# Strided attention with an expert layer on one core: the first sixteen weight loads issued as four loads of 32 partitions each

## The chip, the cores and the metric

The kernel runs on one core of one Trainium2 chip. The metric is the device time of one execution in microseconds (us). Before the change three runs took 869.03, 870.39 and 871.68 us; their median, 870.39 us, is the time that the change is held against.

## What is computed

```python
# q, k, v: (8, 8, 576, 64) float32;  w_in: (512, 2048), w_out: (2048, 512), both float64
scores = (1/8) * q @ k.T                      # per batch and head
mask   = local band of 32      for heads 0..3
         same position mod 32  for heads 4..7    # both causal
attn   = softmax(where(mask, scores, -1e9));  x = (attn @ v) -> (4608 tokens, 512)
h = x @ w_in;  g = h * clip(h + 3, 0, 6) / 6;  out = g @ w_out
```

The weights arrive as 8-byte numbers, so a block of 128 rows by 512 columns is 512 KB in memory.

## The kernel before

All work is written as operations of a planner (class `Plan`): each has an engine, an estimated cost, a due time and the tiles that it reads and writes. `emit` simulates the engines with these numbers and fixes the order in which each engine issues its operations; on the chip every engine then runs its list strictly in that order, waiting on semaphores where an input is not there yet.

A batch is worked on as four pairs of heads (`pair`). Batch 0 goes first: q and k are loaded (L491), turned upright by TensorE (L371), scores (L600, L608), softmax on DVE, POOL and ACT, and the product with v (L388, L735) gives x. The v loads of batch 0 are made of small pieces (L377, L380, L566). From batch 1 on q and k are loaded in 32-row strips (L357) and transposed by DVE (L533). The expert layer of batch 0 (`ffn(0)`) starts as soon as x and the first weights are there: `first_product` (L856 to L858) makes `ph`, ACT and DVE apply the gate (L776, L779), ACT and POOL split the result in a high and a low part (L790, L794), and `mm2` (L833 to L835) adds into `acc`. Later batches use a scheme with fewer products, on the same weights.

The weights come in 32 blocks (`weight_part`, k = 0 to 31): four of w_in (`rawi`), four of w_out (`rawo`), four of w_in and so on. Each is loaded by one DMA on SP's queue (`load`, L273) into a tile of 128 partitions by 1024 32-bit words. ACT then reads it twice (`high` L281, `low` L285), DVE joins the parts (`join` L289), and ACT or POOL write the high part (L303, L305) and POOL the low part (L308). The same place is reused for the result. The first sixteen blocks (k < 16) are loaded early: four before the v loads of the second and fourth pair, the other twelve right behind these; behind the twelve, SP issues the q and k strips of batch 1.

Each DMA of SP tells its landing on one of eight semaphores, taken in turn (DMAHW0 to DMAHW7 in the orders below). SP issues a DMA only when the one that used this semaphore before, eight DMAs earlier, has landed. The DMAs of SP that are issued stand in line for the core's 16 DMA engines.

The lines that fix a weight load:

```python
raw = new(wp, key, [P, TOK, 2], I32, f"raw{name}")
nc.sync.dma_start(raw, src.bitcast(I32).rearrange("p (n t) -> p n t", t=2))
...
op("SP", 0.53, load, writes=[key], due=..., early=7.0 if k < 16 else due - 30.0, ...)
```

Of the kernel before, what the change touches and what calls it, by code (L numbers as in the profile page):

```python
# [12 lines left out]
I32 = mybir.dt.int32  # L13
# [6 lines left out]
P = 128  # L20
# [9 lines left out]
TOK = 512  # L30
TURNS = ((0, 2, 1, 3), (2, 0, 3, 1)) + ((0, 2, 1, 3),) * 6
AHEAD = 27.0
OPEN = 6.0
HIENG = {"ACT": 0.63, "POOL": 0.7}

# [24 lines left out]
class Plan:  # L60
# [12 lines left out]
    def op(self, engine, us, fn, reads=(), writes=(), due=0.0, room=0.0, mode="", after=0.0, take=None, give=None, early=0.0):  # L73
        n = len(self.ops)
        before = set()
        for k in reads:
            if k in self.wrote:
                before.add(self.wrote[k])
            self.used.setdefault(k, []).append(n)
        for k in writes:  # L80
            if k in self.wrote:
                before.add(self.wrote[k])
            before.update(self.used.pop(k, ()))
            self.wrote[k] = n
        before.discard(n)
        how = engine if isinstance(engine, dict) else {engine: us}
        self.ops.append((how, fn, before, due, room, mode, after, take, give, early))
        return n
# [85 lines left out]
def attention_ffn(ctx: ExitStack, tc, q, k, v, w_in, w_out, out):  # L174
    nc = tc.nc
# [21 lines left out]
    op = plan.op  # L197
    tiles = {}

    def new(pool, key, shape, dtype, name):  # L200

        tag = "_".join(str(x) for x in key)
        t = tiles[key] = pool.tile(shape, dtype, tag=tag, name=name)
        return t
# [52 lines left out]
    def wkey(w, g, i):  # L257
        return ("w", w, g, i)

    def weight_part(k, w, g, i):  # L260
        key = wkey(w, g, i)
        fc = FQ * g if w == "i" else FQ * g + i + 1
        due = T0 + fc * TILE / NFC - 5.0 + 0.01 * k
        fkey = ("x", 1, 1 - (k // 2 % 2 if k < 20 else 0), k % 2)
        name = f"{w}{g}{i}"

        def load():
            if w == "i":
                src = w_in[i * P:(i + 1) * P, g * TOK:(g + 1) * TOK]
            else:  # L270
                src = w_out[(g * FQ + i) * P:(g * FQ + i + 1) * P, :]
            raw = new(wp, key, [P, TOK, 2], I32, f"raw{name}")
            nc.sync.dma_start(raw, src.bitcast(I32).rearrange("p (n t) -> p n t", t=2))  # L273

        def bits():
            raw = tiles[key]
            return raw.rearrange("p n t -> p (n t)")[:, :TOK]

        def high():
            f = new(xp, fkey, [P, TOK], I32, f"f{name}")  # L280
            nc.scalar.activation(f.bitcast(F32), tiles[key][:, :, 1].bitcast(F32), AF.Prelu, scale=2.0 ** -112, alpha=2.0 ** 32)  # L281

        def low():
            raw = tiles[key].bitcast(U16).rearrange("p n (t u) -> p n t u", u=2)[:, :, 0, 1]
            nc.scalar.activation(bits(), raw, AF.Copy, scale=2.0 ** -13, bias=2.0 ** -14 - 0.5)  # L285

        def join():
            f = tiles[fkey]
            nc.vector.scalar_tensor_tensor(out=f, in0=f, scalar=3, in1=bits(),  # L289
                                           op0=ALU.logical_shift_left, op1=ALU.bitwise_or)  # L290

        def whole():
            f = tiles[fkey].bitcast(F32)
            return f if w == "i" else f.rearrange("p (h e d) -> p h d e", h=2, d=2)

        def part(x):
            t = tiles[key][:, x]
            return t if w == "i" else t.rearrange("p (h d e) -> p h d e", h=2, d=2)

        def hi(e):  # L300
            new(wp, key, [P, 2, TOK], F32R, f"w{name}")
            if e == "ACT":
                nc.scalar.copy(part(0), whole())  # L303
            else:
                nc.gpsimd.tensor_copy(part(0), whole())  # L305

        def lo():
            nc.gpsimd.tensor_tensor(out=part(1), in0=whole(), in1=part(0).bitcast(F32), op=ALU.subtract)  # L308

        op("SP", 0.53, load, writes=[key], due=-49 + 0.01 * k if k < 4 else -48.4 + 0.01 * k if k < 6 else -2 + 0.1 * k if k < 16 else due - 20.0, early=7.0 if k < 16 else due - 30.0, after=1.6 if k < 16 else 1.25)  # L310
        op("ACT", 0.68, high, reads=[key], writes=[fkey], due=due - 5, room=LATE + 1.0)
        op("ACT", 0.68, low, writes=[key], due=due - 5)
        op("DVE", 1.05, join, reads=[key], writes=[fkey], due=due - 3)
        op(HIENG, 0, hi, reads=[fkey], writes=[key], due=due - 2)
        op("POOL", 1.3, lo, reads=[fkey, key], writes=[key + ("lo",), key], due=due - 1)
# [124 lines left out]
    def pair(g):  # L440
# [37 lines left out]
        for x in "qk":  # L478
# [55 lines left out]
            op("SP", 3.4 if b > 4 else 2.8, load, writes=[nkey], due=due - 35, early=due - 45, after=2.0)  # L534
            op("DVE", 0.8 if loc else 1.25, tr, reads=[nkey, "plain"], writes=[tkey[x]], due=due - 18, early=max(due - AHEAD, T0 + OPEN), room=LATE)

# [1002 lines left out]
    for n, part in enumerate(parts):  # L1539
        weight_part(n, *part)  # L1540
# [63 lines left out]
```

## Time and profile before

| | |
|---|---|
| median of three runs | 870.39 us (869.03 to 871.68) |
| the profiled execution, its own time | 871.98 us |
| its span, first to last instruction | 870.2 us |
| TensorE (PE) busy | 847.4 us, 97% of the span |
| DVE, ACT, POOL busy | 539.0, 558.9, 616.6 us |
| moved by DMA | 179.12 MB, mean 206 GB/s |

The rows of the profile are from the profiled execution, and its 871.98 us is 1.59 us above the median. PE is matrix multiplication, PEld its weight load, SPq the queue of DMA issues on SyncE. A row of the timeline is a run of like instructions on an engine: start, length, engine, line, operation, output and input, count, and in brackets the idle time before it with what ended that. The length of an SPq row is the time that issuing took, not the transfer.

### The profile page before, as it was taken

The page shows a single profiled execution, that of the slowest core. Times are in us where ns is not written, and L with a number is a line of the kernel's source. Part 1 is how long each engine was busy: PE and PEld are TensorE (multiplying, and loading weights), DVE is VectorE, ACT ScalarE, POOL GpSimd, SP SyncE. Part 2 cuts the span into 40 slices and gives each one's busy share as a digit, 9 for nine tenths or more (in the row PEclk, how much of TensorE's full clock was granted, in tenths as well). Part 3 has the DMA queues.
Part 4 walks back from the last instruction along what each step waited for, and adds up shares of the span by engine and source line. Part 5 has one row for each costly group of instructions (what it writes and reads, how often), then busy time and mean ns, then how long its engine had stood idle before and what let it go on. Part 6 is the DMA issues. An engine that isn't in the chain of part 4 may idle for free.

```text
span 870.2 us, 18946 instructions
## 1 busy us (share of the span) xinstructions
PE 847.4 (97%) x6962; PEld 683.8 (79%) x6962; DVE 539.0 (62%) x898; ACT 558.9 (64%) x1246; POOL 616.6 (71%) x606
## 2 busy tenths in 40 slices
PE   8889999999999999999999999999999999999996
PEld 6667777887888788888888878788888778888884
DVE  5688878344454538454546664466767888555586
ACT  3687657678778865877677965776744645454441
POOL 4688877587547799766676994465975987767673
PEclk9999999999999999999999999999999999999998
DMA  8968723898984455898999897877666667866636
GB/s 194 330 138 233 234 41 73 210 281 245 279 234 108 128 129 141 233 266 233 269 277 289 274 301 214 237 204 189 183 202 193 185 180 222 240 202 192 183 122 145
DMA packets 323308, 179.12 MB, mean 206 GB/s; under 512 B 182864, under 2 KB 300368, under 8 KB 323216
## 3 DMA queue, kind: packets, MB, share of 16 engines
q1 hardware_dynamic: 318564, 176.27, 71.5%
q10 hardware_dynamic: 4652, 1.64, 0.9%
q8 instruction: 55, 0.90, 0.4%
q14 instruction: 37, 0.30, 0.1%
HBM read 136.97 MB, written 40.89 MB: 204 GB/s over the span
## 4 chain that ended last, share of the span: by engine, by line
PE 82%; DMA 5%; POOL 5%; DVE 4%; ACT 2%; issue 1%; SPq 0%; POOLq 0%; DVEq 0%; ACTq 0%
PE P L1129 8%; PE P L1130 8%; PE P L1131 8%; PE cP L1452 5%; PE cP L1453 5%; PE cP L1454 5%; PE acc L833 5%; PE ph L856 5%; PE ph L857 4%; PE ph L858 4%; PE acc L835 4%; PE acc L834 4%; PE acc L1214 3%; PE acc L1215 3%; PE acc L1216 3%; PE pv L399 2%
## 5 line engine op out<-in xcount | busy, mean ns | idle before, releaser
L1470 DVE SCALAR_TENSOR_TENSOR C<-cP,C 128x512 f32<-128x512 f32 x96 | 65.7, 687 | 40.4 <-PE cP L1454 39.5
L794 POOL TENSOR_TENSOR gl<-u,gh 128x512 fp32r<-128x512 f32 x48 | 65.2, 1361 | 33.3 <-ACT gh L790 17.1
L1141 DVE TENSOR_TENSOR G<-P,G 128x512 f32<-128x512 f32 x64 | 44.0, 689 | 65.6 <-PE P L1131 53.2
L1129 PE MATMUL P<-B_T,wr 128*128 128x512 f32 x192 | 76.1, 396 | 3.9 <-ACT G L1136 2.3
L833 PE MATMUL acc<-wo,gh 128*128 128x512 f32 x192 | 77.2, 402 | 0.0
L835 PE MATMUL acc<-wo,gl 128*128 128x512 f32 x192 | 75.2, 392 | 0.3 <-POOL gl L794 0.2
L834 PE MATMUL acc<-wo,gh 128*128 128x512 f32 x192 | 74.9, 390 | 0.0
L1130 PE MATMUL P<-B_T,wr 128*128 128x512 f32 x192 | 74.8, 390 | 0.0
L1131 PE MATMUL P<-B_T,wr 128*128 128x512 f32 x192 | 74.8, 390 | 0.0
L1136 ACT COPY G<-P 128x512 f32<-128x512 f32 x64 | 37.6, 587 | 52.2 <-PE P L1131 51.7
L1367 POOL TENSOR_TENSOR sp<-G,sp 128x512 fp32r<-128x512 f32 x34 | 47.6, 1411 | 24.6 <-ACT sp L1363 22.5
L665 POOL TENSOR_TENSOR e<-e,st 128x144 f32<-128x144 f32 (+1 forms) x64 | 44.9, 704 | 20.7 <-DVE st L661 15.2
L779 DVE SCALAR_TENSOR_TENSOR u<-u,ph 128x512 f32<-128x512 f32 x48 | 32.8, 684 | 38.0 <-ACT u L776 37.8
L856 PE MATMUL ph<-x,wi 128*128 128x512 f32 x128 | 52.5, 410 | 2.3 <-ACT x L426 1.2
L857 PE MATMUL ph<-x,wi 128*128 128x512 f32 x128 | 50.8, 397 | 1.4 <-DVE x L429 0.8
L700 ACT COPY atloc<-e 32x192 f32<-32x192 f32 x144 | 50.8, 353 | 1.9 <-DVE e L690 0.3
L776 ACT ACTIVATE u<-ph,three 128x512 f32<-128x512 f32 x48 | 33.0, 687 | 28.1 <-PE ph L858 27.8
L858 PE MATMUL ph<-x,wi 128*128 128x512 f32 x128 | 50.8, 397 | 0.0
L644 DVE TENSOR_REDUCE st<-e 128x8 f32<-128x144 f32 (+1 forms) x64 | 25.6, 412 | 35.8 <-POOL e L640 35.6
L1129 PE MATMUL P<-B_B,wr 128*128 128x512 f32 x120 | 47.1, 392 | 0.0
L1130 PE MATMUL P<-B_B,wr 128*128 128x512 f32 x120 | 46.8, 390 | 0.0
L1129 PEld LDWEIGHTS P<-B_T,wr 128*128 128x128 f32 x192 | 36.0, 188 | 13.7 <-ACT G L1136 3.6
(604 smaller groups left out, 2672.6 us busy)
## 6 DMA issues: line engine op xcount, KB each, us to landing
wr<-dA SPq DMA_DIRECT2D x72, 256.0 KB
or<-do SPq DMA_DIRECT2D x32, 512.0 KB
wr<-dSu SPq DMA_DIRECT2D x48, 256.0 KB
wr<-dSv SPq DMA_DIRECT2D x48, 256.0 KB
or<-do SPq DMA_DIRECT2D x48, 256.0 KB
rawi<-in_moe_w_in_dram SPq DMA_DIRECT2D x16, 512.0 KB
rawo<-in_moe_w_out_dram SPq DMA_DIRECT2D x16, 512.0 KB
do<-wo SPq DMA_DIRECT2D x16, 512.0 KB
```

The lines of the kernel that those rows point to most:

```text
L700: nc.scalar.copy(at[PAD * (a + h):PAD * (a + h) + PAD, :, rows], e[rows, :, PAD * h:PAD * h + PAD])
L794: (nc.vector if tail else nc.gpsimd).tensor_tensor(out=to, in0=src(), in1=tiles[gk[0]].bitcast(F32), op=ALU.subtract)
L833: nc.tensor.matmul(acc, gh, woh, start=fc == 0, stop=False)
L834: nc.tensor.matmul(acc, gh, wol, start=False, stop=False)
L835: nc.tensor.matmul(acc, gl, woh, start=False, stop=end)
L856: nc.tensor.matmul(ph, wih, xh, start=n_ == 0, stop=False)
L857: nc.tensor.matmul(ph, wih, xl, start=False, stop=False)
L858: nc.tensor.matmul(ph, wil, xh, start=False, stop=n_ == NCC - 1)
L1129: nc.tensor.matmul(ph, wh, xh, start=fresh and k == 0, stop=False, skip_group_check=not fresh)
L1130: nc.tensor.matmul(ph, wh, xl, start=False, stop=False, skip_group_check=not fresh)
L1131: nc.tensor.matmul(ph, wl, xh, start=False, stop=k == 1, skip_group_check=not fresh)
L1470: nc.vector.scalar_tensor_tensor(out=tiles[ck], in0=tiles[bank], scalar=1.0 / 6.0, in1=tiles[ck], op0=ALU.mult, op1=ALU.add)
```

## The change

`CHOP = 4` is new. For the first sixteen weight blocks the load is a loop over four quarters of 32 partitions, each a DMA of its own (128 KB instead of 512 KB). For the other sixteen blocks `step` is 128 and one DMA is issued as before. The planner's cost of a load on SP goes from 0.53 to 1.6 us for these sixteen.

```diff
+CHOP = 4
...
             raw = new(wp, key, [P, TOK, 2], I32, f"raw{name}")
-            nc.sync.dma_start(raw, src.bitcast(I32).rearrange("p (n t) -> p n t", t=2))
+            step = P // CHOP if k < 16 else P
+            for p0 in range(0, P, step):
+                nc.sync.dma_start(raw[p0:p0 + step], src[p0:p0 + step].bitcast(I32).rearrange("p (n t) -> p n t", t=2))
...
-        op("SP", 0.53, load, writes=[key], due=..., early=7.0 if k < 16 else due - 30.0, after=1.6 if k < 16 else 1.25)
+        op("SP", 0.4 * CHOP if k < 16 else 0.53, load, writes=[key], due=..., early=7.0 if k < 16 else due - 30.0, after=1.6 if k < 16 else 1.25)
```

Lines below the loop move down by three (L273 is L276 after, L357 is L360). Line and buffer numbers aside, the lists of PE, DVE, ACT and POOL are the same, row for row, before and after; on SP the only rows that differ are the sixteen loads.

On SP, the first four weight loads and what stands behind them; `rawi00` is the block of w_in with group 0 and row block 0, `v0_10` and `v0_3` are v tiles of batch 0. Before:

```order
L566 DMA v0_2_242<-in_v_dram 18x2x512 x4
L273 DMA rawi00_333<-in_moe_w_in_dram 128x1024
L273 DMA rawi01_335<-in_moe_w_in_dram 128x1024
L273 DMA rawi02_357<-in_moe_w_in_dram 128x1024
L273 DMA rawi03_359<-in_moe_w_in_dram 128x1024
L377 DMA v0_10_260<-in_v_dram 32x64
```

and after:

```order
L569 DMA v0_2_242<-in_v_dram 18x2x512 x4
L276 DMA rawi00_333<-in_moe_w_in_dram 32x1024 x4
L276 DMA rawi01_358<-in_moe_w_in_dram 32x1024 x4
L276 DMA rawi02_403<-in_moe_w_in_dram 32x1024 x4
L276 DMA rawi03_429<-in_moe_w_in_dram 32x1024 x4
L380 DMA v0_10_260<-in_v_dram 32x64
```

Four issues have become sixteen, in the same place.

On SP, the end of the twelve later loads and the strips of batch 1 (`qn1_2`, `kn1_2`: third pair), with the semaphores that each issue waits for. Before:

```order
L273 DMA rawo12_591<-in_moe_w_out_dram 128x1024 [waits DMAHW2_49]
L273 DMA rawo13_597<-in_moe_w_out_dram 128x1024 [waits DMAHW3_49]
L357 DMA qn1_2_692<-in_q_dram 32x18x32 [waits DMAHW4_49,PE_49]
L357 DMA qn1_2_692<-in_q_dram 32x18x32 [waits DMAHW5_49]
L357 DMA qn1_2_692<-in_q_dram 32x18x32 [waits DMAHW6_49]
L357 DMA qn1_2_692<-in_q_dram 32x18x32 [waits DMAHW7_49]
L357 DMA kn1_2_730<-in_k_dram 32x18x32 [waits DMAHW0_49,PE_49]
```

and after:

```order
L276 DMA rawo13_934<-in_moe_w_out_dram 32x1024 [waits DMAHW2_49]
L276 DMA rawo13_934<-in_moe_w_out_dram 32x1024 [waits DMAHW3_49]
L360 DMA qn1_2_953<-in_q_dram 32x18x32 [waits DMAHW4_49,PE_49]
L360 DMA qn1_2_953<-in_q_dram 32x18x32 [waits DMAHW5_49]
L360 DMA qn1_2_953<-in_q_dram 32x18x32 [waits DMAHW6_49]
L360 DMA qn1_2_953<-in_q_dram 32x18x32 [waits DMAHW7_49]
L360 DMA kn1_2_982<-in_k_dram 32x18x32 [waits DMAHW0_49,PE_49]
```

The strips keep their semaphores (48 more DMAs are six full turns of the eight), but the eight DMAs ahead of them are now two blocks, where they were eight.

On ACT, the first readers of a weight block. Before:

```order
L720 COPY at64_195<-pe0_01_582 128x288 [waits PE_49]
L281 ACTIVATE fi00_680<-rawi00_333 128x512 [waits DMAHW2_49]
L285 ACTIVATE rawi00_333<-rawi00_333 128x512 [waits Activation_49]
L281 ACTIVATE fi01_689<-rawi01_335 128x512 [waits DMAHW3_49]
L426 CAST x0_00_702<-pv0_00_638 128x288 [waits PE_49]
```

and after:

```order
L723 COPY at64_195<-pe0_01_579 128x288 [waits PE_49]
L284 ACTIVATE fi00_683<-rawi00_333 128x512 [waits DMAHW4_49,DMAHW5_49,DMAHW3_49,DMAHW2_49]
L288 ACTIVATE rawi00_333<-rawi00_333 128x512 [waits Activation_49]
L284 ACTIVATE fi01_697<-rawi01_358 128x512 [waits DMAHW6_49,DMAHW7_49,DMAHW1_49,DMAHW0_49]
L429 CAST x0_00_705<-pv0_00_636 128x288 [waits PE_49]
```

A reader waits for four landings where it waited for one; the same holds for DVE's `join` and POOL's first writer.

## Rows read from the trace of the kernel before

**Rows 1.** The windows view: three stretches of the span. Columns: stretch, its length, busy us of PE, PEld, DVE, ACT, POOL (instructions), granted TensorE clock as a share of full speed, mean busy share of the 16 DMA engines, GB/s that they moved.
```profile
0.00:60.00 60.00, 51.18 (x927) 38.93 (x928) 41.03 (x92) 36.44 (x81) 36.02 (x60) 0.94 0.84 231
60.00:860.00 800.00, 794.25 (x6030) 643.57 (x6029) 494.62 (x803) 522.48 (x1166) 580.57 (x547) 1.00 0.72 205
```
**Rows 2.** The waits view for PE in the first 60 us: instruction that waited, what it waited for, us in total, times, longest.
```profile
PE ps L600 <- issue: 2.5, 2, 1.3
PE pe L371 <- issue: 2.1, 1, 2.1
PE ph L856 <- ACT x L426: 1.2, 1, 1.2
PE ph L857 <- DVE x L429: 0.8, 2, 0.5
```
**Rows 3.** The timeline of SP's queue, merged and in narrow windows: weight loads, v loads and strips. Columns: start us, us that issuing took, then the DMA and its count.
```profile
16.95 2.10 SPq L273 DMA_DIRECT2D rawi<-in_moe_w_in_dram  x4
19.09 0.68 SPq L377 DMA_DIRECT2D v<-in_v_dram  x1
28.02 0.32 SPq L566 DMA_DIRECT2D v<-in_v_dram  x1
28.38 1.77 SPq L273 DMA_DIRECT2D rawo<-in_moe_w_out_dram  x4
34.70 0.33 SPq L273 DMA_DIRECT2D rawo<-in_moe_w_out_dram  x1
35.92 0.33 SPq L273 DMA_DIRECT2D rawo<-in_moe_w_out_dram  x1
38.77 9.25 SPq L357 DMA_DIRECT2D qn<-in_q_dram  x4
50.81 0.50 SPq L357 DMA_DIRECT2D kn<-in_k_dram  x1
53.83 0.52 SPq L366 DMA_DIRECT2D vloc<-in_v_dram  x1
60.56 1.95 SPq L357 DMA_DIRECT2D qn<-in_q_dram  x4
```
**Rows 4.** The waits view for SP's queue from 16 to 48 us (columns as in group 2).
```profile
SPq L273 <- DMA rawo<-in_moe_w_out_dram: 3.6, 4, 1.5
SPq L357 <- DMA rawi<-in_moe_w_in_dram: 3.0, 3, 1.2
```
**Rows 5.** The windows view again (columns as in group 1).
```profile
10.00:12.00 2.00, 2.00 (x67) 2.00 (x64) 1.13 (x2) 1.31 (x3) 0.00 (x0) 1.00 0.87 214
24.00:28.00 4.00, 3.17 (x85) 2.95 (x89) 2.06 (x5) 1.59 (x4) 0.49 (x2) 0.61 1.01 281
40.00:44.00 4.00, 4.00 (x93) 2.98 (x91) 2.55 (x7) 3.12 (x8) 4.00 (x7) 1.00 1.03 417
56.00:60.00 4.00, 4.00 (x13) 3.17 (x12) 2.81 (x4) 3.06 (x6) 3.33 (x3) 0.62 0.06 9
57.00:60.00 3.00, 3.00 (x10) 2.36 (x10) 2.12 (x3) 2.41 (x5) 2.33 (x3) 0.66 0.00 0
```
**Rows 6.** The chain of waits, one piece: start, us, and the DMA whose issue to landing it is (the fourth weight block).
```profile
18.72 8.58 DMA rawi<-in_moe_w_in_dram
```
**Rows 7.** The timeline of ACT: first readings (L281) of the weight blocks 1, 4, 5 and 9, in the order of loading.
```profile
27.30 0.68 ACT L281 ACTIVATE fi<-rawi 128x512 f32<-128x512 f32 x1
39.30 0.67 ACT L281 ACTIVATE fi<-rawi 128x512 f32<-128x512 f32 x1
42.81 0.67 ACT L281 ACTIVATE fo<-rawo 128x512 f32<-128x512 f32 x1
50.30 0.70 ACT L281 ACTIVATE fi<-rawi 128x512 f32<-128x512 f32 x1
```
**Rows 8.** The timeline of DVE, POOL and PE from 59 to 69 us: where the strips of batch 1 are read, and what stands behind.
```profile
59.17 1.36 DVE L533 STREAM_TRANSPOSE qplain<-qn 128x576 f32<-128x576 f32 x1
60.36 0.69 DVE L289 SCALAR_TENSOR_TENSOR fi<-fi,rawi 128x512 int32<-128x512 int32 x1
60.97 1.33 DVE L533 STREAM_TRANSPOSE kplain<-kn 128x576 f32<-128x576 f32 x1
62.17 0.60 POOL L305 CAST wi<-fi 128x512 fp32r<-128x512 f32 x1
64.55 1.27 PE L608 MATMUL ps<-kplain,qplain 64*32 64x18 f32 x128
67.27 1.28 POOL L794 TENSOR_TENSOR gl<-u,gh 128x512 fp32r<-128x512 f32 x1
68.61 0.19 PEld L835 LDWEIGHTS acc<-wo,gl 128*128 128x128 f32 x1 [0.48 <-POOL gl L794]
```
**Rows 9.** The DMA view of two short stretches, 22.2 to 24 and 33.2 to 34.4 us: instruction transfers (packets, MB, share of the 16 engines' time).
```profile
q8 instruction: 1, 0.02, 3.7%
q8 instruction: 1, 0.02, 4.9%
```
**Rows 10.** The timeline of PE at its idle times before 36 us (columns as in group 3; in brackets the idle time before).
```profile
24.83 2.14 PE L371 MATMUL pe<-ident,e 96*64 96x96 f32 x19 [2.10 <-issue]
35.55 0.42 PE L600 MATMUL ps<-kt,qt 64*64 64x36 f32 x11 [1.13 <-issue]
```
**Rows 11.** The chain of waits near 46 us: a piece in which ACT's sequencer does nothing but wait for a semaphore (start, us, line).
```profile
45.99 0.02 ACTq L281
```

More of the change, by code (lines that the diff above doesn't have):

```diff
@@ L308, in lo @@
             nc.gpsimd.tensor_tensor(out=part(1), in0=whole(), in1=part(0).bitcast(F32), op=ALU.subtract)
-        op("SP", 0.53, load, writes=[key], due=-49 + 0.01 * k if k < 4 else -48.4 + 0.01 * k if k < 6 else -2 + 0.1 * k if k < 16 else due - 20.0, early=7.0 if k < 16 else due - 30.0, after=1.6 if k < 16 else 1.25)
+        op("SP", 0.4 * CHOP if k < 16 else 0.53, load, writes=[key], due=-49 + 0.01 * k if k < 4 else -48.4 + 0.01 * k if k < 6 else -2 + 0.1 * k if k < 16 else due - 20.0, early=7.0 if k < 16 else due - 30.0, after=1.6 if k < 16 else 1.25)
         op("ACT", 0.68, high, reads=[key], writes=[fkey], due=due - 5, room=LATE + 1.0)
```

## The prediction

> **What bounds the kernel now.** I read the windows first, then PE's waits, SP's queue and, last, the engines around the places where a load is read. The windows [rows 1] say where time can be lost at all: PE works 794.25 of the 800 us from 60 to 860, so that stretch has 5.75 us of idle time, while the first 60 us have 60 - 51.18 = 8.8. The sixteen loads that change are issued between 17 and 38 us. A loss there is a loss at the end, since PE has no idle time later in which to make it good; a gain there is worth at most a part of 8.8 us. What PE waits for in that stretch [rows 2] is no weight load: 4.6 us in which it waits for nothing that the profile shows, and some 2 us for ACT and DVE, of which the rows of group 2 show why: x of batch 0 was not yet split.
>
> SP's queue [rows 3, 4] shows the loads. The first four are issued in 2.10 us from 16.95, the next from 28.38. From the fifth of the twelve on, SP waits for landings, and its issues tell the speed of the transfers: 34.70 and 35.92 are 1.22 us apart, each at the landing of the block eight places ahead. So 512 KB take 1.22 us, and a quarter 0.31. The window from 40 to 44 agrees: the engines are full (1.03) and move 417 GB/s [rows 5], by which 131 KB take 0.31 us. In short: in this stretch the transfers are the bound of the loads, SP waits for them, and PE waits for neither.
>
> **The change, part by part.**
>
> *Issue time on SP.* 16 issues become 64. No row shows the issue of a 32-partition DMA with rows of 4 KB. Below it lies the smallest DMA, 18 x 2 rows: 0.32 us, and 0.36 to the next one's start at 28.38. Above it lies the same line with four times the rows: four in 1.77 us, 0.44 each [rows 3]. I take 0.40, nearer to the first by its count of rows; bounds 0.36 and 0.44, as long as SP sets the pace.
>
> *The first four blocks.* 16 x 0.40 = 6.4 us instead of 2.10, so the v loads behind them are issued 4.3 us later than 19.09. The ten v issues then took until 28.38, 9.3 us, much of it under a full queue; with the queue emptier part of the 4.3 comes back. The twelve later blocks begin between 28.4 and 32.7; I take 31.4. A load has landed some 2.5 us after its issue: the last one of group 3's stretch was issued at 53.83, and from 57 on nothing moves [rows 3, 5], so 3.2 at most. Block 1 is there at 16.95 + 1.6 + 2.5 = 21.1 and is read at 27.30; block 4 at 25.9, where it landed at 18.72 + 8.58 = 27.30 before, and is read at 39.30 [rows 6, 7]. Cost 0; the cover is that ACT comes to them late.
>
> *The twelve blocks.* 48 x 0.40 = 19.2 us, to 50.6. Each block takes 1.6 us where its transfer needs 1.22, so the engines run a little dry. Block 5 lands at 31.4 + 1.6 + 2.5 = 35.5 and is read at 42.81; block 9 at 41.9 and is read at 50.30 [rows 7]. Cost 0, with 7 to 8 us to spare.
>
> *What is queued behind them.* The strips of batch 1 started at 38.77 and their last issue ended at 50.81 + 0.50 = 51.3 [rows 3], because they stood behind full transfers. Now they start at 50.6; four took 1.95 us where nothing was in the way, so eight end at about 54.6. The q strips land at 50.6 + 2.0 + 2.5 = 55.1 and the k strips at 57.1. DVE reads them at 59.17 and 60.97 [rows 8]: 4 us to spare. Cost 0. This is the place where the change decides: what is late next is DVE's transpose of q, then the join of a weight block at 60.36, and through it POOL. The spare is gone when a quarter takes (60.97 - 2.5 - 4.0 - 31.4) / 48 = 0.48 us instead of 0.40. SP's next strips, at 60.56, wait for that transpose anyway, so from there on the queue is as before.
>
> *More waits.* ACT, DVE and POOL wait for four landings instead of one: 16 x 3 = 48 more on each. Such a wait, already fulfilled, shows 0.02 us on ACT's sequencer [rows 11], so 1.0 us on each engine if nothing covered it; they are taken while the engine still works on the instruction before. I take 0.2 on the path, bounds 0 and 1.0.
>
> *The speed of a quarter's transfer* is the unknown that matters. The whole blocks say 0.31 us. The other end is the window from 10 to 12 us [rows 5], when loads of batch 0 ran that cover 64 to 96 partitions: the engines were 0.87 busy and moved 214 GB/s, half of 417. At that rate 131 KB take 0.61 us. These loads have packets of 2 KB and less, the quarters have those of the whole blocks (4 KB), from the same tensors, in the same queue; so the whole block is the nearer row, and SP's 0.40 stays the pace. The end 0.61 is kept for the range.
> [...]
>
> *Sum.* 0 + 0 + 0 + 0.2. The profiled execution took 871.98 us (span 870.2 and 1.8 around it); 872.2 by its count. It stood 1.59 us above the median, so the median goes from 870.39 to 870.6 us.
>
> **The rivals.**
>
> *Slower: the quarters move at half speed and the strips come late.* At 0.61 us per quarter SP, never more than eight DMAs ahead, is held by the landings. The last quarter lands at about 31.4 + 2.5 + 47 x 0.61 = 62.6. The fourth q strip is issued when the 44th quarter has landed (60.2) and lands near 62.7, the last k strip near 65.1. DVE's transposes at 59.17 and 60.97 [rows 8] are 3.5 and 4.1 us late; the k transpose ends at 66.5 and PE's scores, at 64.55 now, start 1.9 late. The join at 60.36 stands behind the q transpose, POOL's 62.17 behind the join, and POOL's `gl` at 67.27 is what PE already waits for at 68.61 (0.48 us). So PE loses 2 to 4 us, about 3: 873.4. After such idle times the granted clock has been low: 0.61 from 24 to 28, after an idle time of 2.10 us, and 0.62 from 56 to 60 [rows 5, 10], each worth 4 x 0.39 = 1.6 us; once more of that gives 875.0. For it: the 214 GB/s. Against it: the packet size, and 4 us of spare that a pace of 0.48 must first use up. The point from which it decides is that pace.
>
> *Faster: PE gets its instructions sooner.* PE's idle times without a releaser, 2.5 and 2.1 us [rows 2], fall together with transfers of instructions on the same engines, one of 0.02 MB in each of the two stretches looked at [rows 9, 10]. Before, up to eight whole blocks stand in the engines' queues, now eight quarters. If that halves these idle times, 2.3 us come back, and with the 1.6 us of the low clock behind the longest of them 3.9: 866.7. Against it: the engines are as full as before while the quarters run, with the same packets.
>
> *The waits are not covered.* The 48 more waits on each engine cost their 1.0 us where DVE and ACT feed PE: 871.4, still inside what can be told from no change.
>
> That the change does something else than it says can be left out: the orders of all five engines are the same but for the loads.
>
> **How the numbers follow.** I count 0.3%, 2.6 us, as about what a measurement of this kernel can tell from no change. The forecast has 0.54, uncovered waits 0.06, half speed 0.30, instructions sooner 0.10. Of the half-speed case 0.06 ends below 873.0 and counts as no change; the other 0.24 is slower. So 0.10 faster, 0.66 the same, 0.24 slower. The likeliest is 870.6. The range goes down to 868.8, which is the forecast less the spread of the three runs and a little of the faster case, and up to 874.8, which takes in the half-speed case with most of a low-clock stretch.
>
> **What would show it.** Right: SP's sixteen first issues end near 23.4 and the 48 later ones near 50, 0.36 to 0.44 us apart; the engines run at 320 to 360 GB/s between 32 and 48; the first strips are issued near 50.6 and DVE's first transpose still starts near 59.2 without an idle time that a DMA ended; PE's 60 to 860 stays near 794 busy of 800. Wrong: issues about 0.6 us apart that wait for landings, an engine share near 1.0 at 215 GB/s, a transpose of q that starts after 61, and new idle time of PE between 64 and 70. If PE's idle times before 36 us become shorter, the second rival is at work.

## The result and the profile after

| | before | after |
|---|---|---|
| median | 870.41 us (13 runs, 869.03 to 874.27) | 876.46 us (13 runs, 873.54 to 878.59) |
| ratio after to before, with its 95% interval | | 1.0058 (1.0043 to 1.0072) |
| profiled execution: own time, span | 871.98, 870.2 us | 877.54, 875.8 us |

The changed kernel is 0.58% slower by the ratio on record; the two medians lie 0.70% apart. The forecast (870.6) and its range (868.8 to 874.8) are wrong: the first rival happened, and it cost more than it was given. Line numbers of the changed kernel are three higher than before (L273 is now L276).

The windows view of the changed kernel (columns as in [rows 1]):

```profile
0.00:60.00 60.00, 52.58 (x932) 38.60 (x932) 42.05 (x91) 36.94 (x83) 35.59 (x61) 0.97 0.87 207
60.00:860.00 800.00, 788.68 (x5998) 639.54 (x5997) 488.86 (x794) 521.33 (x1164) 576.86 (x546) 1.00 0.73 206
40.00:44.00 4.00, 4.00 (x84) 3.02 (x83) 3.99 (x5) 2.46 (x5) 2.98 (x5) 1.00 1.02 235
44.00:52.00 8.00, 6.49 (x48) 4.47 (x46) 6.91 (x15) 6.27 (x14) 5.36 (x5) 0.79 1.05 240
68.00:72.00 4.00, 3.04 (x132) 2.25 (x132) 3.11 (x5) 1.78 (x4) 3.24 (x3) 0.50 0.91 141
72.00:80.00 8.00, 8.00 (x66) 6.32 (x69) 6.31 (x17) 5.25 (x10) 8.00 (x10) 0.82 0.85 239
```

Two things are to be seen. From 40 to 44 us the engines are as full as in [rows 5] (1.02 against 1.03) and move 235 GB/s instead of 417. And PE, against [rows 1], is busy 1.40 us more in the first 60 us, but 5.57 us less from 60 to 860.

The timeline of SP's queue after (columns as in [rows 3]):

```profile
16.08 10.27 SPq L276 DMA_DIRECT2D rawi<-in_moe_w_in_dram  x16
...
32.74 8.57 SPq L276 DMA_DIRECT2D rawo<-in_moe_w_out_dram  x16
41.36 9.00 SPq L276 DMA_DIRECT2D rawi<-in_moe_w_in_dram  x16
50.53 8.55 SPq L276 DMA_DIRECT2D rawo<-in_moe_w_out_dram  x16
59.39 1.95 SPq L360 DMA_DIRECT2D qn<-in_q_dram  x4
61.60 2.63 SPq L360 DMA_DIRECT2D kn<-in_k_dram  x4
```

The first sixteen quarters take 10.27 us to issue. The other 48 take from 32.74 to 59.39, 26.65 us or 0.555 each, and the strips of batch 1, issued from 38.77 to 51.3 before [rows 3], start at 59.39.

The chain of waits after (start, us, what; a DMA piece is the time from issue to landing):

```profile
42.75 0.42 SPq L276
43.17 0.04 issue
43.22 5.09 DMA rawi<-in_moe_w_in_dram
48.31 0.02 issue
48.33 4.39 DMA rawi<-in_moe_w_in_dram
52.72 0.02 issue
52.74 4.39 DMA rawo<-in_moe_w_out_dram
57.12 0.02 issue
57.14 4.40 DMA rawo<-in_moe_w_out_dram
```

Up to 43 us SP sets the pace: an issue of 0.42 and 0.04 to the next, 0.46 a quarter. From there on the landings do: a piece of 4.40 us is eight quarters in flight, so 0.55 each, which is 131 KB at 240 GB/s. The pieces of both weights take as long (4.39 and 4.40), although a row of w_in starts 16 KB behind the one before and a row of w_out 4 KB behind it: where the rows lie in memory makes no difference here.

The timelines of DVE and PE, where the strips are read (columns as in [rows 8], in brackets the idle time before). Before, of the gate `u` behind the k transpose and of PE's first `acc`:

```profile
62.09 0.73 DVE L779 SCALAR_TENSOR_TENSOR u<-u,ph 128x512 f32<-128x512 f32 x1
60.36 0.39 PE L833 MATMUL acc<-wo,gh 128*128 128x512 f32 x1
```

And after:

```profile
65.11 1.23 DVE L536 STREAM_TRANSPOSE qplain<-qn 128x576 f32<-128x576 f32 x1 [6.66 <-DMA qn<-in_q_dram]
66.18 0.67 DVE L292 SCALAR_TENSOR_TENSOR fi<-fi,rawi 128x512 int32<-128x512 int32 x1
67.14 1.24 DVE L536 STREAM_TRANSPOSE kplain<-kn 128x576 f32<-128x576 f32 x1 [0.29 <-DMA kn<-in_k_dram]
68.22 0.69 DVE L782 SCALAR_TENSOR_TENSOR u<-u,ph 128x512 f32<-128x512 f32 x1
58.88 0.39 PE L836 MATMUL acc<-wo,gh 128*128 128x512 f32 x1
68.96 0.79 PE L836 MATMUL acc<-wo,gh 128*128 128x512 f32 x1 [6.06 <-DVE u L782]
70.53 1.46 PE L611 MATMUL ps<-kplain,qplain 64*32 64x18 f32 x128
```

DVE stands still for 6.66 us at the transpose of q, which began at 59.17 in [rows 8]. Behind it in DVE's fixed order stand a join, the transpose of k and the gate `u`; PE has done its products by 62.9 and waits 6.06 us for that `u`. After that idle time its granted clock is low: the share is 0.50 from 68 to 72 and 0.82 from 72 to 80. PE was busy for 3.04 and 8.00 us of these, so 3.04 x 0.50 + 8 x 0.18 = 3.0 us of work is lost. The scores (L611) start at 70.53 instead of 64.55 [rows 8].

The timeline of PE after, at its idle times before 36 us (as [rows 10]):

```profile
18.12 1.02 PE L603 MATMUL ps<-kplain,qplain 64*64 64x36 f32 x55 [0.26 <-issue]
23.75 0.93 PE L374 MATMUL pe<-ident,e 96*64 96x96 f32 x12 [0.75 <-POOL e L668]
26.94 0.77 PE L391 MATMUL pv<-at,v 64*64 64x32 f32 x36 [0.66 <-issue]
34.83 0.90 PE L374 MATMUL pe<-ident,e 96*64 96x96 f32 x12 [0.25 <-issue]
```

The idle time of 2.10 us without a releaser [rows 10] is gone; near it stands one of 0.75, in which PE waits for POOL's `e`. So the balance has a gain in it. Idle: 1.40 less before 60 us, 5.57 more after. Clock: 0.97 instead of 0.94 over the first 60 us gives 1.8 back, 3.0 is lost behind the wait. 5.57 - 1.40 + 3.0 - 1.8 = 5.4 us; the span grew by 5.6.

### The profile page after: what moved, and what is told of

It reads as the page before. It is cut to its first block, busy times and chain, and to the rows that moved or that the text cites. A ratio compares the mean times of both kernels' runs of the same rounds, so it can differ in the third digit from the quotient of the medians.

```text
span 875.8 us, 19052 instructions
## 1 busy us (share of the span) xinstructions
PE 849.2 (97%) x6962; PEld 684.4 (78%) x6962; DVE 540.0 (62%) x898; ACT 558.3 (64%) x1246; POOL 614.1 (70%) x606
## 4 chain that ended last, share of the span: by engine, by line
PE 84%; DMA 5%; POOL 3%; SPq 3%; DVE 3%; issue 1%; ACT 1%; DVEq 0%; POOLq 0%
PE P L1132 8%; PE P L1134 8%; PE P L1133 8%; PE acc L836 5%; PE cP L1455 5%; PE cP L1457 5%; PE cP L1456 5%; PE ph L859 5%; PE acc L838 5%; PE acc L837 5%; PE ph L861 4%; PE ph L860 4%; PE acc L1217 3%; PE acc L1219 3%; PE acc L1218 3%; PE pv L402 2%
## 5 line engine op out<-in xcount | busy, mean ns | idle before, releaser
L1144 DVE TENSOR_TENSOR G<-P,G 128x512 f32<-128x512 f32 x64 | 44.0, 689 | 65.1 <-PE P L1134 52.7
L782 DVE SCALAR_TENSOR_TENSOR u<-u,ph 128x512 f32<-128x512 f32 x48 | 32.7, 684 | 38.4 <-ACT u L779 38.2
L860 PE MATMUL ph<-x,wi 128*128 128x512 f32 x128 | 50.6, 396 | 2.2 <-DVE x L432 2.2
L836 PEld LDWEIGHTS acc<-wo,gh 128*128 128x128 f32 x192 | 36.3, 189 | 14.7 <-DVE u L782 6.5
```

Source lines behind the costliest of these rows:

```text
L836: nc.tensor.matmul(acc, gh, woh, start=fc == 0, stop=False)
L860: nc.tensor.matmul(ph, wih, xl, start=False, stop=False)
```

## The experiments

All start from the changed kernel. Theory 1: what is slow is the piece that lies in a part of the partitions, and its cost comes through the strips. Theory 2: it is the number and the size of the loads.

| run | pieces of the first blocks | median, us | ratio to before (95%) | last piece of qn landed | PE waits for `u` |
|---|---|---|---|---|---|
| the change | 16 blocks, 4 x 32 partitions | 876.46 | 1.0058 (1.0043, 1.0072) | 64.98 | 6.06 |
| halves | 16 blocks, 2 x 64 partitions | 873.25 | 1.0018 (1.0002, 1.0033) | 60.84 | 0.30 |
| spread | 16 blocks, 4 x 32, every fourth partition | 882.59 | 1.0127 (1.0103, 1.0150) | 71.44 | 9.84 |
| columns | 16 blocks, 4 x 128 columns | 874.90 | 1.0031 (1.0017, 1.0046) | 63.45 | 3.71 |
| strips first | as the change, strips ahead of block 8 | 876.72 | 1.0053 (1.0034, 1.0072) | 45.28 | none |
| column halves | 16 blocks, 2 x 256 columns | 870.40 | 0.9988 (0.9971, 1.0006) | 52.89 | none |
| first four | blocks 0 to 3, 4 x 32 partitions | 869.00 | 0.9977 (0.9963, 0.9992) | 56.13 | none |
| other twelve | blocks 4 to 15, 4 x 32 partitions | 872.50 | 1.0010 (0.9995, 1.0024) | 60.67 | 3.01 |
| alternate | as the change, order 0, 64, 32, 96 | 874.59 | 1.0033 (1.0017, 1.0048) | 62.48 | 4.03 |
| first eight | blocks 0 to 7, 4 x 32 partitions | 870.58 | 0.9996 (0.9982, 1.0011) | 58.25 | 0.34 |
| first four, columns | blocks 0 to 3, 4 x 128 columns | 870.16 | 0.9987 (0.9974, 1.0000) | 54.49 | none |

The kernel before had medians of 870.41 to 871.80 us beside these runs; the ratios are to that. Its last piece of qn landed at 51.43. A landing is the last signal of the load's semaphore in the trace.

### Halves, spread and columns

```diff
 # halves
-            step = P // CHOP if k < 16 else P
+            step = P // 2 if k < 16 else P
 # spread
+            step = CHOP if k < 16 else 1
+            for p0 in range(step):
+                nc.sync.dma_start(raw[p0::step], src[p0::step]...)
 # columns
+            words = ...            # the block as 32-bit words
+            step = TOK // CHOP if k < 16 else TOK
+            for n0 in range(0, TOK, step):
+                nc.sync.dma_start(raw[:, n0:n0 + step], words[:, n0:n0 + step])
```

> The first sixteen weight blocks go as two loads of 64 contiguous partitions (256 KB each) instead of four of 32. Theory 1 (a piece that lies in part of the partitions moves at about half speed, whatever its size): two loads have the same speed as four, 235 to 250 GB/s while the blocks move, some 1.1 us per load; the last block lands at about 63 us, qplain is read by DVE at about 65, PE loses its 6 us between 62 and 69, and the time is that of the change, 875 to 878. Theory 2 (each load has a cost of its own, so that 64 loads are too many, be it on SP or in the number of loads in flight): half as many loads cost half as much; 12 blocks then take about 12 x 2 x 0.55 = 13 us, the strips land at about 52 us, before DVE wants them, and the time is 869 to 872.

> The first sixteen weight blocks go as four loads of 32 partitions each as in the change, with the same number of loads, bytes and rows of 4 KB, but a load takes every fourth partition (0, 4, 8 and so on) and not 32 that lie side by side. Theory 1 (the half speed comes from which partitions a piece covers): the pieces move at 300 GB/s or more, and SP's issue sets the pace at 0.40 to 0.46 us per piece; the last quarter lands by about 57 to 59 us, the strips at 60 to 61, which is what DVE can bear, and the time is 869 to 873. Theory 2 (the number of loads or their size): nothing changes against the change, 875 to 878, with 235 to 250 GB/s between 40 and 60 us. [...]

> The first sixteen weight blocks go as four loads of all 128 partitions by a quarter of the columns each (128 rows of 1 KB, 128 KB), with the same number of loads and bytes as in the change. Theory 1 (part of the partitions makes the half speed): the speed is above 300 GB/s, unless the shorter rows cost some of it; the issue of 0.40 to 0.46 us per piece sets the pace, strips by 60 to 61 us, 869 to 873. Theory 2 (number or size of the loads): as the change, 875 to 878.

The windows view from 44 to 52 us, of halves (with the stretch from 40 to 44), spread and columns in turn:

```profile
40.00:44.00 4.00, 4.00 (x30) 2.97 (x26) 1.40 (x5) 3.14 (x9) 3.93 (x6) 1.00 1.04 254
44.00:52.00 8.00, 7.92 (x127) 6.00 (x125) 7.26 (x17) 7.71 (x16) 4.72 (x7) 1.00 1.03 250
```
```profile
44.00:52.00 8.00, 5.10 (x46) 3.18 (x45) 7.05 (x13) 5.46 (x11) 5.00 (x5) 1.00 0.67 200
```
```profile
44.00:52.00 8.00, 6.40 (x52) 4.29 (x50) 7.86 (x16) 7.15 (x14) 4.34 (x5) 1.00 0.77 239
```

Neither theory came through whole. Halves move at 250 GB/s with full engines, as theory 1 said, but the time is not the 875 to 878 that it gave: the strips land at 60.84 us, 4 us sooner than with quarters, and PE loses only 0.30 there. What halves lose against the kernel before (1.0018) is not shown; in its profiled run PE's clock is 0.91 over the first 60 us, where it was 0.94. Spread and columns don't keep the engines full (0.67 and 0.77), so there the transfer is no bound, and yet they lose. The bound is taken to be SP, whose issues come no faster: in spread one takes 0.59 us and sixteen from 46.51 take 10.14 (0.63 each), in columns 0.43 and about 0.5 to the next. In spread weight blocks come late too: ACT waits 3.2 us in all for four of them.

The timeline of SP's queue, first of spread, then of columns:

```profile
46.51 2.50 SPq L276 DMA_DIRECT2D rawi<-in_moe_w_in_dram  x4
```
```profile
32.71 8.99 SPq L277 DMA_DIRECT2D rawo<-in_moe_w_out_dram  x16
41.75 8.64 SPq L277 DMA_DIRECT2D rawi<-in_moe_w_in_dram  x16
50.43 7.91 SPq L277 DMA_DIRECT2D rawo<-in_moe_w_out_dram  x16
58.43 2.43 SPq L361 DMA_DIRECT2D qn<-in_q_dram  x4
```

In columns 48 issues take 58.43 - 32.71 = 25.72 us, 0.536 each. So there are two limits side by side, and for quarters of 32 neighbouring partitions they lie close together: 0.46 us by SP's bare issue, some 0.53 with its interruptions (0.54 in the changed kernel itself, for the sixteen issues from 32.74 to 41.36, none of which waited for a landing), 0.55 by the transfer. One of the interruptions, in the changed kernel, is a pair of issues of 1.49 us where 0.88 is usual, with an instruction transfer in the same stretch (the timeline of SP's queue from 43.1 us, and the DMA view from 42.5 to 44 us):

```profile
42.75 1.49 SPq L276 DMA_DIRECT2D rawi<-in_moe_w_in_dram  x2
```
```profile
q8 instruction: 1, 0.02, 5.0%
```

### Column halves

```diff
-            step = TOK // CHOP if k < 16 else TOK      # columns
+            step = TOK // 2 if k < 16 else TOK
```

> Two loads for each of the first sixteen blocks, as in the run of halves (256 KB each), but each takes all 128 partitions and half of the columns (2 KB rows) instead of 64 partitions and all columns. Number and size of the loads are the same, the partitions alone differ. Theory 1, as it stands after the first four runs (a contiguous piece of 32 or 64 partitions moves at half speed because its rows take 265 to 291 ns each instead of 159; beside it SP can't issue pieces of 128 KB faster than one in about 0.52 us, which is why columns and spread lose too): here neither limit binds, the speed from 40 us on is above 350 GB/s, the strips land at about 53 to 56 us as before, and the time is 869.5 to 872. Theory 2 (two loads in place of one cost something by their number): the strips land at about 60 us and the time is that of the halves, 872 to 874.

The windows view of column halves:

```profile
40.00:44.00 4.00, 4.00 (x82) 2.93 (x84) 1.53 (x6) 3.12 (x9) 2.99 (x4) 1.00 1.03 383
```

This is the clean pair: two loads of 256 KB per block in both, engines full in both, 383 GB/s with all partitions and 254 in the same window (250 from 44 to 52) with 64 neighbouring ones. The strips land at 52.89 against 60.84 us and the time is 0.9988 against 1.0018, with intervals that just overlap. That the partitions, not number or size, make the transfer slow is shown; what that is worth in time is less firm.

### Strips first

```diff
 # emit: the order of SP alone; the other engines' lists stay
+        at = ...                    # the place of the load of block 8
+        turns[at:at] = strips       # qn and kn of batch 1
```

> The change with its quarters as they are, and one thing moved in SP's order alone: the two strips of batch 1 (qn and kn, four loads each) that stand behind the sixteen blocks stand ahead of the ninth block. The other engines' orders are as in the change. Theory 1 (the loss is the 6 us in which DVE, and behind it PE, waits for these strips, and the slow quarters cost nothing else): the quarters still move at 240 GB/s and the last lands at about 66 us, but the strips land before 50 us, DVE's transposes run at 59 to 61 us and PE's wait of 6.06 us on u goes; the time is 869 to 872. If it falls to below 869, the earlier start of PE in the first 30 us, which the change has too, is a gain of its own. Theory 2 here: late weight blocks or the crowded DMA queues hold PE too, and the time stays above 873.

The timelines of ACT, PE and DVE in this run, and its windows view:

```profile
50.26 0.67 ACT L290 ACTIVATE fi<-rawi 128x512 f32<-128x512 f32 x1 [1.60 <-DMA rawi<-in_moe_w_in_dram]
53.07 0.49 PE L869 MATMUL ph<-x,wi 128*128 128x512 f32 x1 [2.25 <-ACT x L437]
59.98 1.32 DVE L544 STREAM_TRANSPOSE qplain<-qn 128x576 f32<-128x576 f32 x1
61.70 1.36 DVE L544 STREAM_TRANSPOSE kplain<-kn 128x576 f32<-128x576 f32 x1
72.85 0.78 DVE L544 STREAM_TRANSPOSE qplain<-qn 128x576 f32<-128x576 f32 x1 [4.87 <-DMA qn<-in_q_dram]
75.89 1.20 PE L621 MATMUL ps<-kplain,qplain 64*32 64x64 f32 x72 [2.55 <-DVE kplain L544]
```
```profile
56.00:60.00 4.00, 4.00 (x11) 3.14 (x10) 2.00 (x4) 2.72 (x5) 0.72 (x2) 0.50 1.01 241
```

The local part held: the strips are read at 59.98 and 61.70 and PE's wait for `u` is gone. The time did not fall, and "the slow quarters cost nothing else" is refuted. Block 8, pushed back, is now late for ACT (1.60 us), and the next strips, which stand behind all quarters in SP's queue, make DVE wait 4.87 us at 72.85. Behind the first PE loses 2.25 us at 53.07 (0.87 in the change) and runs at 0.50 of its clock, behind the second 2.55 us at 75.89. Up to 860 us PE stands idle for 18.6 us in this run and for 18.7 in the change: the idle time has only moved. The queue as a whole is late; moving one thing ahead hands the delay to the next.

### First four, first eight, other twelve

```diff
-            step = P // CHOP if k < 16 else P
+            step = P // CHOP if k < 4 else P           # first four
+            step = P // CHOP if k < 8 else P           # first eight
+            step = P // CHOP if 4 <= k < 16 else P     # other twelve
```

> Only the first four blocks go as quarters, the other twelve whole. Theory 1 (the loss comes from the strips behind the quarters): SP is some 4 us later after the first four, as in the change, but twelve whole blocks make that up to a landing of the strips at 55 to 57 us, ahead of DVE's 59; no wait of PE on u; 869 to 871.5. If the earlier start of PE in the change (first acc at 58.88 instead of 60.36 us) comes from the first four blocks and lasts, 867.5 to 869. Theory 2 (the first four quarters hold the chip in some other way): 872 or more.

> The first eight blocks go as quarters, the other eight whole: a point between the run with four and the change with sixteen. Theory 1 (the loss is how late the strips land against DVE's turn): from four to sixteen quartered blocks the last piece of qn went from 56.13 to 64.98 us, 0.74 us per block, so with eight it lands at about 59 us, where DVE is ready for it at 57.3 to 58.5; u comes 1 to 2 us later than with four, which PE's work of some 6 us after the first acc still covers: no wait of PE on u above 1 us, 868.5 to 870.5. If the loss grew with the number of quarters from the first on, a third of the way from 869.0 to 876.5: 871 to 872.

> The first four blocks whole, the other twelve as quarters. Theory 1: 48 quarters at 0.55 us run from about 28.4 to 55 us on SP, the strips land at about 60 to 61.5 us, 3 to 4 us sooner than in the change; DVE waits 1 to 3 us for qplain and PE loses little of it: 871.5 to 874.5. Where the whole loss comes with these twelve: 875 to 878.

The timeline of PE in the run of the first four, then in that of the other twelve:

```profile
23.25 0.93 PE L374 MATMUL pe<-ident,e 96*64 96x96 f32 x12 [0.74 <-POOL e L668]
58.10 0.39 PE L836 MATMUL acc<-wo,gh 128*128 128x512 f32 x1
```
```profile
64.56 0.50 PE L836 MATMUL acc<-wo,gh 128*128 128x512 f32 x1 [3.01 <-DVE u L782]
```

The three runs give the price by place. With the first four alone the qn strips land at 56.13, before DVE wants them; PE keeps the shorter idle time near 23 us (0.74 instead of 2.10 [rows 10]), its clock from 24 to 28 us is 1.00 instead of 0.61 [rows 5], and the time is 869.00, ratio 0.9977: faster than before, and the lowest median of this study. With eight the strips land at 58.25, foretold as about 59, and PE waits 0.34; its median, 870.58, lies 0.08 above what was expected, nearer to that than to the 871 to 872 of the other reading, but its interval holds both (a straight line from four to sixteen would give 1.0004). With the other twelve they land at 60.67 and PE waits 3.01. The sum tells more: four alone give -0.23%, twelve alone 0.10%, both together 0.58%, so the loss is not so much per quarter; it sets in when the strips are late. The point is not a fixed time. In halves they land at 60.84 and PE waits only 0.30, because PE itself came to that `acc` at 64.76 us; in the run of the other twelve it came at 61.55.

### Alternate

```diff
-            for p0 in range(0, P, step):
+            for p0 in (0, 64, 32, 96) if k < 16 else (0,):
                 ...
```

> The change with its four quarters issued in the order 0, 64, 32, 96 instead of 0, 32, 64, 96, so that neighbours in the queue lie in different halves of the partitions. If two neighbours in flight can use both halves at once, a row takes well under 291 ns, the pace is then SP's 0.5 us per piece, and the time is 873.5 to 875.5, near that of columns. If they can't, rows stay at 265 to 291 ns, the pace at 0.55 us, and the time at 875 to 878. [...]

The windows view of this run:

```profile
44.00:52.00 8.00, 5.33 (x47) 3.35 (x46) 7.86 (x15) 7.30 (x15) 5.63 (x5) 1.00 0.79 243
```

The same order of speed (243 GB/s) needs 0.79 of the engines instead of 1.05. That neighbours from different halves overlap in part would fit this; by itself it was not shown. Nor is how fast they could go: the sixteen issues from 40.91 us take 8.53, 0.53 each as in columns (0.536), with engines that are not full. So SP's issue is taken to be the bound again, and the time, 874.59, is that of columns, the first of the two expectations.

### First four, columns

```diff
+            step = TOK // CHOP if k < 4 else TOK           # the rest as in columns
```

> Only the first four blocks in pieces, as four loads of all 128 partitions by a quarter of the columns. If the gain of the run with the first four as quarters comes from the pace at which SP issues pieces of 128 KB, behind which less data stands queued ahead of PE's instruction packets (PE's gap 'issue' at 23 to 25 us 0.74 us instead of 2.10, and the next not at half clock), it is here too, whatever partitions the pieces cover: gap below 1 us, 868 to 870. If the gain comes from the slow rows of the partition quarters, which leave DMA bandwidth to others, the gap is back at 1.3 us or more and the time at 870 to 871.5.

The timeline of PE in this run:

```profile
18.60 1.02 PE L604 MATMUL ps<-kplain,qplain 64*64 64x36 f32 x55 [1.06 <-issue]
24.22 0.93 PE L375 MATMUL pe<-ident,e 96*64 96x96 f32 x12 [0.74 <-POOL e L669]
```

The gap near 24 us is 0.74, as with partition quarters, so the shorter gap does not need slow rows; it goes with SP issuing pieces at its own pace. The clock from 24 to 28 us is 1.00 here too. The gap at 18 us shrank only to 1.06 (1.34 before). The time, 870.16, lies 0.16 above the first expectation, in the second one, though the gap is that of the first; its interval overlaps that of the first four: whether partition quarters are better than column quarters here stays open.

## Why the prediction was wrong, step by step

*What bounds the kernel now* held: a wait of PE after 60 us was not made good.

*Issue time on SP* failed in size. 0.40 us was taken, 0.44 was the upper bound; it measured 0.46 from start to start and 0.53 with the interruptions (columns; 0.54 in the changed kernel from 32.74 to 41.36). The latter is above the pace of 0.48 at which the prediction itself saw the spare gone, so this step alone would have brought the time to the upper end of the range: columns and alternate, whose engines were not full (0.77 and 0.79), are at 874.90 and 874.59. The rows used were single issues; what sixteen or more in a row take had to be bounded too.

*The speed of a quarter's transfer* is the step that failed in its choice. 0.31 us was taken from the whole blocks, 0.61 kept as the other end; it is 0.55. The reason given, that quarters have the whole blocks' 4 KB packets, was the wrong likeness: the column halves have packets of 2 KB and move 383 GB/s, the halves have 4 KB and move 250. The nearer row was the window from 10 to 12 us [rows 5], whose loads also covered a part of the partitions; it could not tell by itself, since its packets differed as well, 177 of its 372 being under 512 B. Halves and quarters move 250 and 240 GB/s, 0.60 and 0.58 of the 417 of whole blocks [rows 5], where 0.61 us stood for half. The order of the quarters counts too: in the alternating run the engines' share fell from 1.05 to 0.79 at about the same speed.

*The first four blocks* and *The twelve blocks* held in their cost: no reader of a weight block waits for it in the changed kernel. But sixteen issues took 10.27 us instead of 6.4. The v issues behind them gave most of that back (6.35 us instead of 9.3), so the twelve began at 32.74, the late end of the 28.4 to 32.7 considered, 1.3 us behind the 31.4 taken.

*What is queued behind them* named the right place. With 0.55 a quarter instead of 0.40, plus the 1.3 us, the strips start at 59.39 instead of 50.6; the last q strip then takes 4.0 us from issue to landing (60.97 to 64.98) instead of 2.5, and DVE waits 6.66 us where 4 us of spare were counted.

*More waits*: 0.2 us was taken. No run isolates it; the first four has 12 more landings to wait for and is faster than before.

*Slower: the quarters move at half speed and the strips come late* had the mechanism, and mis-sized its price. Its strips, at 62.7 and 65.1, came at 64.98 and 67.02; that this is near is partly luck, since its pace of 0.61 was too slow and its start of 31.4 too early. It followed the delay through the scores and POOL, for 2 to 4 us; what PE waited for first is `u`, one place behind the k transpose in DVE's order. It starts at 68.22 instead of 62.09, and PE, which had come to it 1.48 us sooner, had too little work to cover that: 6.06 us. The clock behind it cost 3.0 instead of 1.6 us.

*Faster: PE gets its instructions sooner* has its sign beside it: PE's idle times without a releaser shrank, the first `acc` came at 58.88 instead of 60.36 us, and alone (first four) worth 0.23%, about 2.0 us, instead of the 3.9 us given. That the instruction transfers are the cause of the shorter gaps was not tested by itself.

## What to carry to other kernels

When a load is cut into pieces, cut it so that each piece still covers all partitions (two column halves per block moved 383 GB/s and lost nothing, 0.9988; two partition halves moved 254), and count each issue on its queue at the pace of a long row of issues, not of a single one; here both limits, 0.55 and 0.53 us per 128 KB, lay above the 0.48 that the plan could bear. Ask what stands behind the loads in the queue and in its reader's fixed order: no weight block was late here, but eight small loads behind them were, and one gate behind the strips stopped PE. Cutting only the loads whose successors have time to spare kept the gain without the loss (869.00 us, 0.9977).

## What the runs showed of the hardware that was not expected

- Four pieces of 32 partitions that lie four apart cost SP more to issue than four of neighbouring partitions: 0.59 against 0.42 us each, with the same rows of 4 KB. The spread run had engines that were not full (0.67) and was the slowest, 1.0127.
- A full share of the DMA engines did not tell the speed: at 1.02 to 1.05 they moved 235 to 254 GB/s into 32 or 64 neighbouring partitions, 383 and 417 into all of them.
- Quarters issued in the order 0, 64, 32, 96 took less of the engines at about the same speed: a share of 0.79 at 243 GB/s, against 1.05 at 240 in the order of the change.
